# Forget terms in attention: a broadcast row added on the vector engine, or terms of the score product

## The chip, the cores and the metric

One core of one Trainium2 chip runs the whole program. Its engines work from queues of their own and meet through semaphores: TensorE (PE; its weight loads are listed apart as PEld), VectorE (DVE), ScalarE (ACT), GpSimd (POOL) and SyncE (SP), which here issues every DMA. The metric is device time in microseconds (us) for one execution, as the median of several executions. Lower is better.

## The reference

Attention with forget terms for 8 batches of 8 heads, 576 positions, 64 features per head, and behind it a channel mix over 512 features with 1024 hidden ones.

```
s_pos = np.maximum(s, 0.0)
cum = np.cumsum(s_pos, axis=-1)
bias = -(cum[:, :, :, None] - cum[:, :, None, :])
scores = np.where(causal, -1000000000.0, scores + np.minimum(bias, 0.0))
scores = scores - np.max(scores, axis=-1, keepdims=True)
attn = np.exp(scores)
attn = attn / (np.sum(attn, axis=-1, keepdims=True) + 1e-09)
...
xk = mu_k * x + (1.0 - mu_k) * x_prev
xr = mu_r * x + (1.0 - mu_r) * x_prev
k = np.maximum(xk @ w_k, 0.0)
v = k * k @ w_v
r = 1.0 / (1.0 + np.exp(-(xr @ w_r)))
return (r * v).astype(np.float32)
```

`scores` is q times k over the square root of 64. Of the bias a row of scores needs only the part of the key, `cum[key]`: the part of the query is the same along the row and falls out when the row's maximum is taken off. Below the diagonal `min(bias, 0)` is the bias itself. The weights w_k, w_v and w_r arrive as 64-bit floats.

## The kernel before

**The work.** A visit is a pair of heads of one batch. The 576 queries of a head are cut into five tiles: tile 0 has 64 queries, tiles 1 to 4 have 128 each, and tile t sees 64, 192, 320, 448 or 576 keys (QS, QN and KN in the code). Batch 0 goes in two rounds: the four pairs with tiles 0 to 2, which are the first 320 queries (visits of kind A), then the four pairs with tiles 3 and 4 (kind Z). Batches 1 to 7 take all five tiles at once; from batch 3 on two half tiles share a transpose (kind `Paired`, where `front` shifts the columns of tiles 2 and 4 by 64).

**A head.** `scores` makes the products of a tile into one of two PSUM banks `s`. In the first four visits this is a plain float32 product with one term (L719, two instructions each). Behind that the operands are split in two fp32r parts: G holds q's high part over its low part, KH is k's high part twice, KL its low part, and two products, KH by G and KL by G, add up (L730). Tile 4 is wider than a bank and goes in two halves of 288 keys. Then DVE adds the forget row, scales, and keeps the row's minimum of the negated scores (L757, each with a read of its accumulator). It does so in two kinds of pieces: keys left of the diagonal block take the row `cb`, which a DMA has spread from `cum_d` in DRAM over 128 partitions (L682, 288 KB a head), and keys of the diagonal block take `mask`, which POOL makes from `cb` with affine selects (L701). That is 5 pieces for an A head, 5 for a Z head and 10 for a head of all tiles. ACT takes the exponential and its sum (L775), POOL normalises (L791), PE transposes (L837), ACT and DVE split the transposed weights (L866, L870), PE multiplies with v (L986 in the plain visits, L1000 behind).

**The first rows.** `first_sums` spreads s of two heads over all partitions and runs two scans on DVE (L496); `prefix_sums` scans all 64 heads at once (L472) and writes `cum_d`; two DMAs of 480 KB spread the rows of six more heads.

**Loads.** SP loads q and k of each head twice, once for each half of the partitions (L630). ACT and POOL make the parts: KH (L645), KL (L649), G (L656, L660).

**The channel mix** runs over 18 chunks of 256 positions: mixing (L1104, L1111), splits xh and xl (L1133, L1137), hidden products (L1165), gates (L1207), outputs (L1232). Chunk 0 needs the A rounds of all four pairs. Its weights are turned from 64-bit to 32-bit floats and split on ACT, DVE and POOL, in 20 blocks of 512 KB (L548 to L579), spread over the first 110 us.

**The order.** All tasks are recorded with their reads and writes, priced, and put in an order by `Plan`: a list schedule over all engines by due times, twenty passes, the best one kept. So a changed task moves its neighbours too. While PE would idle before the first split score product, `Plan` fills it with small products of the identity (L398).

## Time and profile before

| What | Value |
|---|---|
| median of 3 runs | 860.07 us (859.77 to 861.87) |
| the profiled execution's own time | 860.73 us |
| its span, first to last instruction | 858.9 us |
| granted TensorE clock, mean | 0.998 |
| PE busy | 844.9 us, 98% of the span |
| DVE, ACT, POOL busy | 676.3, 679.2, 494.5 us |
| DMA | 109.04 MB, mean 127 GB/s |

Sums of the prediction are made against the profiled execution (860.73 us around a span of 858.9). A windows row gives a stretch, its length, then for PE, PEld, DVE, ACT and POOL the busy time and number of instructions, the granted clock, the share of time the 16 DMA engines moved data, and GB/s. A timeline row gives start, duration, engine, line, operation, output and inputs. The ends of matmuls are modelled, so a busy PE may still lose some time between them.

### The profile page before, as it was taken

What the parts mean: (1) busy time and instruction counts of PE and PEld (TensorE: products, weight loads), DVE (VectorE), ACT (ScalarE), POOL (GpSimd) and SP (SyncE); (2) the same over time, 40 slices, a digit from 0 to 9 for tenths busy, and PEclk for the clock granted to TensorE, in tenths of its full rate; (3) what the DMA queues carried; (4) which work ended last, traced back from release to release, by engine and by line L of the source; (5) the groups of instructions that cost most, each with busy time, mean ns of one, the idle gap of its engine ahead of it and who ended that gap; (6) DMA issues with size and microseconds to landing.
All of it is one profiled execution on the core that took longest, in us unless ns stands there. A gap on an engine that the chain in (4) does not pass through costs nothing.

```text
span 858.9 us, 18405 instructions
## 1 busy us (share of the span) xinstructions
PE 844.9 (98%) x5541; PEld 748.7 (87%) x5541; DVE 676.3 (79%) x2425; ACT 679.2 (79%) x1850; POOL 494.5 (58%) x854
## 2 busy tenths in 40 slices
PE   9979999999999999999999999999999999999998
PEld 8659789889898898989898989898989989988996
DVE  6988889989877998789878887888888789455431
ACT  3998999999988898789979797978897878445331
POOL 5897899997766757466665566456665652000000
PEclk9999999999999999999999999999999999999999
DMA  8879655564443545335343435252534220210100
GB/s 249 257 236 265 192 164 166 166 184 141 148 136 111 144 124 156 96 112 158 110 128 118 136 104 158 77 149 84 168 98 135 86 92 15 64 33 18 50 26 24
DMA packets 63108, 109.04 MB, mean 127 GB/s; under 512 B 10144, under 2 KB 24480, under 8 KB 63008
## 3 DMA queue, kind: packets, MB, share of 16 engines
q1 hardware_dynamic: 63008, 107.87, 42.7%
q8 instruction: 43, 0.70, 0.3%
q14 instruction: 57, 0.47, 0.2%
HBM read 88.80 MB, written 19.04 MB: 126 GB/s over the span
## 4 chain that ended last, share of the span: by engine, by line
PE 91%; ACT 3%; DMA 2%; DVE 1%; issue 1%; POOL 1%; SPq 0%; ACTq 0%; POOLq 0%; DVEq 0%
PE m L1232 21%; PE m L1165 19%; PE s L730 10%; PE m L1207 10%; PE po L1000 9%; PE t L837 9%; PE t L1232 2%; PE po L398 2%; PE po L986 2%; PE s L1165 2%; PE t L1165 2%; PE t L1000 1%; PE t L937 1%; PE s L719 1%; DMA w_v<-in_moe_w_v 1%
## 5 line engine op out<-in xcount | busy, mean ns | idle before, releaser
L1165 PE MATMUL m<-xh,w_k 128*128 128x256 f32 x976 | 200.3, 286 | 0.0
L775 ACT ACTIVATE W<-W,nm 128x448 f32<-128x448 f32 (+4 forms) x320 | 179.9, 563 | 25.2 <-DVE nm L757 22.4
L1232 PE MATMUL m<-w_v,kh 128*128 128x512 f32 x528 | 188.1, 406 | 0.0
L791 POOL TENSOR_SCALAR W<-W,rinv 64x64 f32<-64x64 f32 (+4 forms) x320 | 164.3, 532 | 12.6 <-DVE rinv L820 10.6
L1165 PEld LDWEIGHTS m<-xh,w_k 128*128 128x128 f32 x976 | 158.8, 189 | 1.4 <-DVE kl L1194 0.2
L837 PE MATMUL t<-ident,W 128*128 128x128 f32 (+1 forms) x736 | 134.7, 276 | 6.4 <-ACT ph L866 2.7
L1165 PE MATMUL m<-xl,w_k 128*128 128x256 f32 x488 | 139.7, 286 | 0.0
L649 POOL TENSOR_TENSOR KL<-raw,KH 128x576 fp32r<-128x576 f32 x64 | 91.6, 1432 | 80.1 <-ACT KH L645 75.4
L870 DVE TENSOR_TENSOR pl<-t,ph 128x512 fp32r<-128x512 f32 x224 | 107.1, 485 | 12.7 <-ACT ph L866 10.7
L837 PEld LDWEIGHTS t<-ident,W 128*128 128x128 f32 (+1 forms) x736 | 89.3, 137 | 27.0 <-ACT ph L903 5.2
L1232 PEld LDWEIGHTS m<-w_v,kh 128*128 128x128 f32 x528 | 98.1, 189 | 15.3
L730 PE MATMUL s<-KH,G 128*64 128x64 f32 (+2 forms) x360 | 110.7, 312 | 0.3 <-DVE nm L757 0.3
L757 DVE CUSTOM_DVE_ANT_0 W<-s,cb 128x64 f32<-128x64 f32 (+1 forms) x244 | 92.1, 381 | 17.9 <-PE s L730 15.4
L1232 PE MATMUL m<-w_v,kl 128*128 128x512 f32 x264 | 105.7, 400 | 0.0
L730 PE MATMUL s<-KL,G 128*64 128x64 f32 (+3 forms) x360 | 105.5, 297 | 0.0
L866 ACT CAST ph<-t 128x512 fp32r<-128x512 f32 x224 | 93.1, 424 | 12.5 <-PE t L837 10.5
L660 POOL TENSOR_TENSOR G<-raw,G 64x576 fp32r<-64x576 f32 (+1 forms) x64 | 85.8, 1341 | 27.6 <-issue 10.2
L1111 DVE SCALAR_TENSOR_TENSOR xp<-x,mu,xp 128x256 f32<-128x256 f32 (+3 forms) x184 | 76.3, 415 | 25.0 <-ACT xp L1104 22.5
L1104 ACT ACTIVATE xp<-x,mu 128x256 f32<-128x256 f32 (+3 forms) x184 | 77.6, 422 | 21.4 <-DMA x<-x_d 12.1
L1165 PEld LDWEIGHTS m<-xl,w_k 128*128 128x128 f32 x488 | 92.2, 189 | 0.8 <-DVE xl L1137 0.3
L1207 PE MATMUL m<-w_r,xh 128*128 128x512 f32 x264 | 92.6, 402 | 0.0
L757 DVE CUSTOM_DVE_ANT_0 W<-s,mask,nm 128x128 f32<-128x128 f32 x256 | 86.7, 344 | 3.1 <-POOL mask L701 0.5
(154 smaller groups left out, 1934.0 us busy)
## 6 DMA issues: line engine op xcount, KB each, us to landing
raw<-in_k SPq DMA_DIRECT2D x128, 144.0 KB, 3.2
cb<-cum_d SPq DMA_DIRECT2D x64, 288.0 KB, 3.6
raw<-in_q SPq DMA_DIRECT2D x112, 144.0 KB, 3.7
out<-g SPq DMA_DIRECT2D x36, 256.0 KB, 2.6
vn<-in_v SPq DMA_DIRECT2D x28, 320.0 KB, 3.3
x_d<-xT SPq DMA_DIRECT2D x28, 288.5 KB, 2.5
x<-x_d SPq DMA_DIRECT2D x11, 514.0 KB, 4.6
w_k<-in_moe_w_k SPq DMA_DIRECT2D x8, 512.0 KB, 5.5
```

The lines of the kernel that those rows point to most:

```text
L649: lambda k=k, kh=kh, kl=kl: nc.gpsimd.tensor_tensor(out=kl.get(), in0=k.get(), in1=f32(kh.get()), op=ALU.subtract),
L730: lambda x=x, K=K: nc.tensor.matmul(ps.get()[:m, :w], G.get()[:, q0 : q0 + m], K.get()[:, k0 : k0 + w], start=x == 0, stop=x == 1,),
L757: lambda a=a, e=e, row=row, i=i, to=to: nc.vector.tensor_tensor_reduce(out=to(), in0=ps.get()[:m, a - k0 : e - k0], in1=row()[:m, a:e], sc ...
L775: lambda: nc.scalar.activation(W.ap[:m, :n], W.ap[:m, :n], AF.Exp, bias=nm.get()[:m, 3 * t + mi : 3 * t + mi + 1], scale=-1.0, accum_out=s ...
L791: lambda: nc.gpsimd.tensor_scalar(out=to.ap[:m, c : c + n], in0=W.ap[:m, :n], scalar1=rinv.get()[:m, t : t + 1], scalar2=1.0, op0=ALU.mult ...
L837: lambda: nc.tensor.transpose(ps.get()[0:m, place : place + P], pt[t].ap[:, k0 + front(t, tiles) : k0 + front(t, tiles) + m], ident.ap,),
L866: act(lambda: nc.scalar.copy(strips(ph), src()), [ps], [(ph, k) for k in ks], n * m)
L870: lambda: nc.vector.tensor_tensor(out=strips(pl), in0=src(), in1=f32(strips(ph)), op=ALU.subtract),
L1000: lambda: nc.tensor.matmul(po.get()[: P if both else 64, at + q0 - base : at + q0 - base + m], V.get()[:, kb, 2 * j : 2 * j + (2 if both e ...
L1165: lambda u=u, f=f, c=c, n=n, w=w, x=x: nc.tensor.matmul(ps.get()[:, u * CT : (u + 1) * CT], weight["k", c, f // 4].get()[:, w, f % 4 * P : ...
L1207: lambda c=c, n=n, x=x, w=w: nc.tensor.matmul(ps.get(), x.get()[:, c, ts], weight["r", c, 0].get()[:, w], start=c == 0 and n == 0, stop=c ...
L1232: lambda f=f, n=n, x=x, w=w: nc.tensor.matmul(ps.get(), x.get()[:, f, ts], weight["v", f, 0].get()[:, w], start=f == 0 and n == 0, stop=f ...
```

## The change

The forget row is no longer added from SBUF by DVE. In the first four visits (the first 320 queries of batch 0) PE adds it to the score: products whose weights are one head's forget terms, one column of them repeated, and whose moving operand is `till`, a triangle of ones (L739 in the changed kernel). A tile of w keys takes two such products (the high and the low part) for each block of 128 keys: 2, 4 and 6 for tiles 0, 1 and 2, so 12 for an A head and 96 in all. For the rest the running sums of all heads are cut into three fp32r parts and kept in DRAM (`cum3_d`), and three rows of them are loaded under k's 64 rows, against three rows of ones under the low part of q. The two score products are now K by QQ (q's high part twice, k's high and low part) and KB by QL (64 rows of k, rounded, and the 3 rows), with 67 rows in the second (L761). So there are as many score products as before.

With the forget term in the sum, DVE adds only a fixed table, `lower` (zeros, and a triangle of large negative numbers), and takes a tile in one piece (L779): 3 pieces for an A head, 3 for a Z head, 6 for a head of all tiles and 8 for a Paired one. The selects on POOL, the rows `cb` and `mask`, and the spreading DMAs go. k is loaded once for both heads of a pair. A copy of 64 rows of k to KB (L703) comes to DVE, one for each of the 64 split heads (the Z and the full ones), and a DMA of 3 rows for each (L687). At the start come five memsets, two subtractions of 64x576 on DVE and two casts of 64x576 on ACT. The planner's constants are unchanged.

```diff
-    cum_d = fixed(dram.tile([B * H, S], F32, name="cum_d"))
+    cum3_d = fixed(dram.tile([B * H, 3, S], F32, name="cum3_d"))
+    lower = fixed(const.tile([P, S], F32, name="lower"))
...
+        parts = [sbuf([B * H, S], x, 1, F32R) for x in ("w_v_2_0", "w_v_3_0", "xh1")]
+        for i, x in enumerate(parts):
+            if i < 2:
+                act(lambda x=x: nc.scalar.copy(x.get(), cum.get()), [cum], [x], S, 90)
+                dve(
+                    lambda i=i, x=x: nc.vector.tensor_tensor(
+                        out=(parts[2] if i else cum).get(), in0=cum.get(), in1=f32(x.get()),
+                        op=ALU.subtract,
+                    ),
+                    [cum, x], [parts[2] if i else cum], S,
+                )
+            dma(
+                lambda i=i, x=x: nc.sync.dma_start(cum3_d.ap[:, 2 - i], f32(x.get())),
+                [x], [(cum3_d, i)], 410,
+            )
...
+    def early_sums():
...
+        till = sbuf([P, n], "xh0", 1, F32R)
+        one = sbuf([P, n], "xl1")
+        rows = sbuf([P, nb, H], "r")
+        parts = sbuf([P, 2, nb, H], "xl0", 1, F32R)
...
+        dve(lambda: nc.vector.memset(one.get(), 1.0), [], [one], n)
+        pool(
+            lambda: nc.gpsimd.affine_select(
+                out=one.get(), in_=one.get(), pattern=[[1, n]], base=0, channel_multiplier=-1,
+                compare_op=ALU.is_ge, fill=0.0,
+            ),
+            [], [one], n, 137,
+        )
...
+            own, other = slice(64 * j, 64 * j + 64), slice(64 - 64 * j, P - 64 * j)
+            QQ, K = (sbuf([P, n], x, 3, F32R) for n, x in ((nq, "G"), (nk, "KH")))
+            QL, KB = (sbuf([P, S], x, 3, F32R) for x in ("QL", "KL"))
+            if made[0] < 3:
+                made[0] += 1
+                ahead(lambda QL=QL: nc.vector.memset(f32(QL.get()[64:67]), 1.0), (QL, 1), S)
+            dma(
+                lambda j=j, KB=KB: nc.sync.dma_start(
+                    f32(KB.get()[64:67, 0:nk]), cum3_d.ap[b * H + 2 * hp + j, :, 0:nk]
+                ),
+                [(cum3_d, i) for i in range(3)], [(KB, 1)], 40,
+            )
...
+                lambda own=own, other=other, K=K: nc.gpsimd.tensor_tensor(
+                    out=K.get()[other], in0=k.get()[own], in1=f32(K.get()[own]), op=ALU.subtract
+                ),
+                [(k, j), (K, j)], [(K, 1 - j)], nk, 210, 2.21, (2 * j, 2 - 2 * j),
+            )
+            dve(
+                lambda own=own, KB=KB: nc.vector.tensor_copy(KB.get()[0:64, 0:nk], k.get()[own]),
+                [(k, j)], [(KB, 0)], nk, 1.92, 150, (2 * j, 0),
+            )
...
+                lambda x=x, QQ=QQ, QL=QL: nc.gpsimd.tensor_tensor(
+                    out=QL.get()[0:64, 0:nq], in0=x.get()[0:64], in1=f32(QQ.get()[0:64]),
+                    op=ALU.subtract,
+                ),
+                [(x, 0), (QQ, 0)], [(QL, 0)], nq, 210, 2.21,
+            )
+            found.append(((QQ, K, P), (QL, KB, 67)))
+        return found
...
-            CB, part = sbuf([P, NK], "cb", 2), 0
-            bias_row = CB.get
-            dma(
-                lambda: nc.sync.dma_start(
-                    CB.get(), cum_d.ap[b * H + h : b * H + h + 1, 0:NK].broadcast_to([P, NK])
-                ),
-                [cum_d], [CB], 819 * NK / S,
-            )
...
-            pool(
-                lambda: nc.gpsimd.affine_select(
-                    out=own(M.get),
-                    in_=own(bias_row),
-                    pattern=[[-1, m]] if n == 1 else [[0, n], [-1, m]],
-                    base=0,
-                    channel_multiplier=1,
-                    compare_op=ALU.is_ge,
-                    fill=MASK * ISCALE,
-                ),
-                [(CB, part)], [(M, k0 > 0)], n * m, 137,
-            )
...
+                parts, till = bias
+                for kb in range(-(-w // P)):
+                    for x in range(2):
+                        pe(
+                            lambda kb=kb, x=x: nc.tensor.matmul(
+                                ps.get()[:m, P * kb : w],
+                                parts.get()[:, x, kb, h : h + 1].broadcast_to([P, m]),
+                                till.get()[:, 0 : w - P * kb],
+                                start=kb == x == 0,
+                                stop=False,
+                            ),
+                            [(parts, x), till], [ps], w - P * kb, m,
+                        )
...
-            for x, K in enumerate((KH, KL) if KL is not None else ()):
+            for x, (G, K, n) in enumerate(() if plain else passes):
                 y = pe(
-                    lambda x=x, K=K: nc.tensor.matmul(
+                    lambda x=x, G=G, K=K, n=n: nc.tensor.matmul(
                         ps.get()[:m, :w],
-                        G.get()[:, q0 : q0 + m],
-                        K.get()[:, k0 : k0 + w],
+                        G.get()[:n, q0 : q0 + m],
+                        K.get()[:n, k0 : k0 + w],
                         start=x == 0,
                         stop=x == 1,
...
-            for a, e in ((k0, min(k0 + w, QS[t])), (max(k0, QS[t]), k0 + w)):
+            off = S - P - QS[t] if QS[t] < k0 + w else -k0
+            last = k0 + w - (f if QS[t] < k0 + w else 0)
+            for a, e, to in ((k0, last, k0 + f), (last, k0 + w, 0)):
                 if a >= e:
                     continue
-                own = a >= QS[t]
-
-                def to(a=a, e=e, own=own):
-                    x = W.ap[:m, a + f : e if own else e + f]
-                    if not (own and f):
-                        return x
-                    return bass.AP(
-                        tensor=x.tensor, offset=x.offset, ap=[x.ap[0], [-P * t, 2], [1, 64]]
-                    )
-
-                bias, row = (M, M.get) if own else (CB, bias_row)
                 dve(
-                    lambda a=a, e=e, row=row, i=i, to=to: nc.vector.tensor_tensor_reduce(
-                        out=to(),
+                    lambda a=a, e=e, to=to, i=i: nc.vector.tensor_tensor_reduce(
+                        out=W.ap[:m, to : to + e - a],
                         in0=ps.get()[:m, a - k0 : e - k0],
-                        in1=row()[:m, a:e],
+                        in1=lower.ap[:m, off + a : off + e],
...
-            loaded[n] = load_turned(q, b, hp, q0, q1), load_turned(k, b, hp, 0, q1)
+            loaded[n] = load_twice(b, hp, q0, q1), load_keys(b, hp, q1, "raw", 4)
...
+    ahead(lambda: nc.vector.memset(lower.ap, 0.0), lower, S)
+    pool(
+        lambda: nc.gpsimd.affine_select(
+            out=lower.ap[:, S - P : S], in_=lower.ap[:, S - P : S], pattern=[[-1, P]], base=0,
+            channel_multiplier=1, compare_op=ALU.is_ge, fill=MASK * ISCALE,
+        ),
+        [], [lower], P, 137,
+    )```

Three places where the order changes. The first is PE's queue in the A rounds; s is a PSUM bank of scores, t one of transposes, xh and xl hold the triangle and the forget terms, KH and kl or kh hold k and q, and ident is the identity. Before:

```order
L837 MATMUL t_418<-ident,W_72 64x128
L719 MATMUL s_218<-KH_125,kh_105 64x64
L837 MATMUL t_418<-ident,W_72 64x128
L986 MATMUL po_87<-ph_143,V_290 128x64
L837 MATMUL t_413<-ident,W_72 128x128
L719 MATMUL s_213<-KH_125,kh_105 128x192
```

And now:

```order
L739 MATMUL s_146<-xh_112,xl_138 128x320
L739 MATMUL s_146<-xh_112,xl_138 128x192 x2
L739 MATMUL s_146<-xh_112,xl_138 128x64 x2
L750 MATMUL s_146<-KH_179,kl_123 128x320
L856 MATMUL t_316<-ident,W_72 128x128 x2
```

Each score product has the running sums ahead of it in its bank, and the first ones of a bank can stand well ahead of the product.

The second is DVE's queue in the first Z heads; cb and mask are the forget rows, W the scores, m and xp banks in which weights are turned, and KL what the changed kernel calls KB. Before:

```order
L757 ISA W_0_71,nm0_241<-s1_213,cb0_162 128x288
L757 ISA nm0_241 128x1
L571 SCALAR_TENSOR_TENSOR xh10_256<-w_r_0_00_610,xp0_325 128x512
L820 RECIPROCAL rinv1_423<-rinv1_423 128x3
L757 ISA W_0_71,nm0_241<-s0_218,cb0_162,nm0_241 128x160
L757 ISA nm0_241 128x1
L757 ISA W_0_71,nm0_241<-s0_218,mask0_184,nm0_241 128x128
L757 ISA nm0_241 128x1
```

And now:

```order
L839 RECIPROCAL rinv1_313<-rinv1_313 128x3
L703 CAST KL0_569<-raw3_433 64x576
L582 TENSOR_SCALAR xp0_307<-xp0_307 128x512
L779 ISA W_1_72,nm1_254<-s1_146,lower_77 64x64
L779 ISA nm1_254 64x1
L589 TENSOR_SCALAR xp0_307<-xp0_307 128x512
L779 ISA W_1_72,nm1_254<-s0_143,lower_77 128x192
L779 ISA nm1_254 128x1
```

A piece of 160 and one of 128 keys are gone as separate instructions, and the copy L703 stands between pieces of the A heads, in front of steps that turn weights (L582, L589).

The third is PE's queue where chunk 0 begins. Before, 18 split score products stand ahead of chunk 0's first hidden product, and the first half of chunk 0's inputs (w_k of rows 0 and 1) follows in one piece:

```order
L730 MATMUL s0_218<-KH0_762,G2_792 128x288
L730 MATMUL s0_218<-KL2_833,G2_792 128x288
L1165 MATMUL m0_197<-xh00_845,w_k_0_00_268 128x256
L1165 MATMUL m0_197<-xl00_851,w_k_0_00_268 128x256
L1165 MATMUL m0_197<-xh00_845,w_k_0_00_268 128x256
L1165 MATMUL m0_197<-xh00_845,w_k_1_00_351 128x256
```

Now 14 stand ahead of it:

```order
L761 MATMUL s1_146<-KH0_683,G2_690 128x288
L856 MATMUL t1_310<-ident_66,W_0_71 128x128
L1184 MATMUL m0_197<-xh00_112,w_k_0_00_344 128x256
L856 MATMUL t0_316<-ident_66,W_0_71 128x128 x3
L1184 MATMUL m0_197<-xl00_138,w_k_0_00_344 128x256
L1184 MATMUL m0_197<-xh00_112,w_k_0_00_344 128x256
```

Chunk 0's first products moved ahead of transposes and score products of the Z heads.

More of the change, by code (lines that the diff above doesn't have):

```diff
@@ new lines, in early_sums @@
+    def early_sums():
+        n = KN[A[-1]]
+        nb = -(-n // P)
+        till = sbuf([P, n], "xh0", 1, F32R)
+        one = sbuf([P, n], "xl1")
+        rows = sbuf([P, nb, H], "r")
+        parts = sbuf([P, 2, nb, H], "xl0", 1, F32R)
+        dma(
+            lambda: nc.sync.dma_start(
+                rows.get(), s_t[0, 0 : nb * P].rearrange("(k p) h -> p k h", p=P)
+            ),
+            [], [rows], 100,
+        )
+        dve(lambda: nc.vector.memset(one.get(), 1.0), [], [one], n)
[6 more added lines that the diff above has]
+        )
+        act(lambda: nc.scalar.copy(till.get(), one.get()), [one], [till], n, 90)
+        act(
+            lambda: nc.scalar.activation(rows.get(), rows.get(), AF.Relu, scale=ISCALE),
+            [], [rows], nb * H, 94,
+        )
+        act(lambda: nc.scalar.copy(parts.get()[:, 0], rows.get()), [rows], [(parts, 0)], nb * H, 90)
+        dve(
+            lambda: nc.vector.tensor_tensor(
+                out=parts.get()[:, 1], in0=rows.get(), in1=f32(parts.get()[:, 0]), op=ALU.subtract
+            ),
+            [rows, (parts, 0)], [(parts, 1)], nb * H,
+        )
+        return parts, till
@@ L635, in load_turned, with ahead @@
         return xs
-    def split_qk(qs, ks):
-        nq, nk = qs[0].n, ks[0].n
-        G = [sbuf([P, nq], "G", 3, F32R) for _ in range(2)]
-        KH, KL = ([sbuf([P, nk], x, 3, F32R) for _ in range(2)] for x in ("KH", "KL"))
-        for j in range(2):
-            k, kh, kl = ks[j], KH[j], KL[j]
-            act(
-                lambda k=k, kh=kh: nc.scalar.copy(kh.get(), k.get()),
-                [(k, 0), (k, 1)], [(kh, 0), (kh, 1)], nk, 90,
+    made = [0]
+    def ahead(emit, what, n):
+        due, plan.due = plan.due, -2.0e5
+        dve(emit, [], [what], n)
+        plan.due = due
@@ new lines, in split_qk @@
+    def split_qk(b, hp, qs, k):
+        nq, nk = qs[0].n, k.n
+        found = []
+        for j in range(2):
+            own, other = slice(64 * j, 64 * j + 64), slice(64 - 64 * j, P - 64 * j)
[10 more added lines that the diff above has]
+            )
+            act(
+                lambda own=own, K=K: nc.scalar.copy(K.get()[own], k.get()[own]),
+                [(k, j)], [(K, j)], nk, 90,
@@ L722, in products @@
                         KH.get()[:, k0 : k0 + w],
-                        start=True,
+                        start=False,
                         stop=True,
@@ L766, in products @@
                     ),
-                    [ps, (bias, t > 0 if own else part)] + ([(nm, (t, i - 1))] if i else []),
+                    [ps, lower] + ([(nm, (t, i - 1))] if i else []),
                     [(W, i), (nm, (t, i))], e - a, extra=143 if i else 78,
@@ L803, in rs @@
             return x.get()[:, tiles[0] : tiles[-1] + 1]
-        if 0 in tiles:
-            mask(64, 0, 1)
-        mask(P, QS[max(1, tiles[0])], len([t for t in tiles if t]))
         for t in tiles:
@@ L1313, in forgetting_attention_then_channel_mix @@
     plan.due = -2.0e5
[L1314 removed]
+    bias = early_sums()
     prefix_sums()
[L1316 to L1326 removed]
     QKs, Vs, early_x = {}, {}, []
@@ L1433 @@
     for name in _INS:
-        a = inputs[name]
+        a = inputs[name.removesuffix("_t")]
+        if name == "s_t":
+            a = a.transpose(0, 2, 1)
         if name in ("q", "k"):
```

86 lines of the change are left out of this document (19 added, 67 removed).

## The prediction

> **What bounds the kernel now.** I read the head of the page first, then the windows by stage, then the chain of waits for prices.
>
> ```profile
> span 858.9 us, 18405 instructions
> PE 844.9 (98%) x5541; PEld 748.7 (87%) x5541; DVE 676.3 (79%) x2425; ACT 679.2 (79%) x1850; POOL 494.5 (58%) x854
> ...
> 0.00:20.00 20.00, 18.18 (x175) 16.64 (x176) 12.56 (x37) 7.72 (x18) 9.90 (x37) 1.00 0.83 239
> 20.00:61.00 41.00, 33.85 (x192) 24.28 (x189) 37.68 (x139) 38.78 (x125) 36.55 (x72) 0.96 0.81 250
> 61.00:90.00 29.00, 28.92 (x195) 25.79 (x195) 24.36 (x68) 26.16 (x64) 23.45 (x29) 1.00 0.97 263
> 90.00:112.00 22.00, 21.52 (x119) 16.68 (x117) 18.90 (x74) 21.30 (x59) 19.91 (x31) 1.00 0.60 171
> 112.00:230.00 118.00, 117.97 (x814) 105.48 (x813) 107.93 (x448) 114.46 (x326) 103.63 (x179) 1.00 0.56 164
> 230.00:700.00 470.00, 469.33 (x3107) 422.12 (x3105) 392.55 (x1474) 398.71 (x1103) 291.78 (x491) 1.00 0.42 122
> 700.00:845.00 145.00, 145.00 (x909) 129.81 (x908) 80.99 (x191) 72.02 (x162) 9.26 (x21) 1.00 0.12 38
> ```
>
> From 112 to 845 us PE stands still for 0.7 of 733 us, at full clock. There the time is the number of columns that PE streams, and a lighter DVE, POOL or DMA buys nothing. The head is another stage: from 20 to 61 us PE is busy for 33.85 of 41, while ACT has 38.78 and DVE 37.68. And part of PE's work in the head is filler; these are the windows of the filler's line alone:
>
> ```profile
> 0.00:20.00 20.00, 15.67 (x159) 14.61 (x160) 1.00 0.83 239
> 20.00:61.00 41.00, 3.98 (x32) 2.63 (x30) 0.96 0.81 250
> ```
>
> So to 61 us, where chunk 0 begins, PE does 18.18 + 33.85 - 15.67 - 3.98 = 32.4 us of real work and has 28.6 us free. Turning the weights and the A rounds on ACT and DVE set the pace. The change has to be priced twice: as PE work wherever PE is full, and as ACT, DVE, POOL and DMA work in the head.
>
> **PE: score products behind the A rounds.** Their number and columns stay, 720 as before; the contraction is 67 rows in every second one. What a column costs is read from long runs of equal products on the chain (start, time, what):
>
> ```profile
> 114.47 0.87 PE t L837 x8
> ...
> 829.87 5.68 PE s L1165 x48
> 843.98 11.18 PE t L1232 x48
> ```
>
> 256 columns take 118 ns and 512 take 233, both with 128 rows, so 0.45 ns a column and some 3 ns an instruction. No row shows a product with 67 rows. The nearest, the two groups of the present score products,
>
> ```profile
> L730 PE MATMUL s<-KH,G 128*64 128x64 f32 (+2 forms) x360 | 110.7, 312 | 0.3 <-DVE nm L757 0.3
> L730 PE MATMUL s<-KL,G 128*64 128x64 f32 (+3 forms) x360 | 105.5, 297 | 0.0
> ```
>
> differ by 15 ns a product, in favour of the second, for equal columns. I take 0 and bound it by 360 x 15 ns = 5.4 us either way, which I think far too wide. Each product has its own weight load before and now, so the second operand adds no loads.
>
> **PE: 96 products of running sums.** An A head has 2 of 64, 2 x (192 + 64) and 2 x (320 + 192 + 64) columns, 1792 in 12 products; eight heads 14336 in 96. That is 14336 x 0.45 + 96 x 3 ns = 6.7 us. Where the small ones are held up by their weight loads, the row of eight transposes above bounds them: each has a load of its own and takes 109 ns, so 96 x 109 ns = 10.5 us at most. I take 6.7, since most columns lie in long products. It lies at about 7 to 50 us, in the 28.6 us that PE has free; the cover is ACT and DVE. If PE were full there it would cost 6.7. On the path: 0, bounds 0 and +6.7. What is queued behind a product that waits for its bank is the transposes and v products of the heads before, as the first piece of order shows.
>
> **DVE.** A piece costs its start-to-start distance:
>
> ```profile
> 5.86 0.50 DVE L465 TENSOR_SCALAR mask<-mask 64x576 f32<-64x576 f32 x1 [5.86 <-DMA mask<-in_s]
> 6.29 0.80 DVE L496 TENSOR_TENSOR_SCAN cb<-raw,raw 128x320 f32<-128x320 f32 x1
> ...
> 18.47 0.35 DVE L757 CUSTOM_DVE_ANT_0 W<-s,cb 128x192 f32<-128x192 f32 x1
> ...
> 18.74 0.34 DVE L757 CUSTOM_DVE_ANT_0 W<-s,mask,nm 128x128 f32<-128x128 f32 x1
> ...
> 19.02 0.35 DVE L757 CUSTOM_DVE_ANT_0 W<-s,mask,nm 128x128 f32<-128x128 f32 x1
> ...
> 41.96 0.47 DVE L757 CUSTOM_DVE_ANT_0 W<-s,cb 128x320 f32<-128x320 f32 x1
> 42.37 0.07 DVE L757 DVE_READ_ACCUMULATOR2_ANT nm<- 128x1 f32 x1
> ```
>
> 192 and 128 keys take 0.27 + 0.28 us, one piece of 320 takes 0.41: a merge saves 0.14. In the head there are 2 merges in each of 16 A and Z heads and 4 in about two full heads: 40 x 0.14 = 5.6 us. Against it stand the copies L703, twelve by the time the last weights are turned (counted in the order). Of one element for one, 64x576, the row above takes 0.43 us start to start. The weight steps of 128x512 take 0.68 us, which is the upper bound. So 12 x 0.43 = 5.2, up to 8.2. Net -0.4, bounds -0.4 and +2.6. Two scans of 0.80 go and five memsets and two subtractions come, about as much as that and 2 us more by the same rows; they stand before 20 us, where DVE has 7.4 us free. Behind 112 us DVE loses or gains a fraction of a us per head under a full PE: nothing.
>
> **ACT, POOL, DMA.**
>
> ```profile
> L649 POOL TENSOR_TENSOR KL<-raw,KH 128x576 fp32r<-128x576 f32 x64 | 91.6, 1432 | 80.1 <-ACT KH L645 75.4
> L701 POOL TENSOR_SCALAR_AFFINE_SELECT mask<-cb 64x64 f32<-64x64 f32 (+1 forms) x124 | 50.9, 427 | 16.0 <-DMA cb<-cum_d 10.1 <-DVE cb L496 3.7 <-DVE nm L757 0.3
> L645 ACT CAST KH<-raw 128x576 fp32r<-128x576 f32 x64 | 43.0, 672 | 1.4 <-DMA raw<-in_k 0.9 <-PE s L730 0.6
> ...
> PEld t L837 <- POOL W L791: 1.6, 3, 0.8
> PE t L837 <- POOL W L791: 0.9, 2, 0.6
> ...
> DMA packets 11577, 22.68 MB, mean 252 GB/s; under 512 B 1820, under 2 KB 5959, under 8 KB 11566
> raw<-in_k SPq DMA_DIRECT2D x20, 144.0 KB, 4.8
> cb<-cum_d SPq DMA_DIRECT2D x8, 288.0 KB, 5.6
> w_v<-cum_d SPq DMA_DIRECT2D x2, 480.0 KB, 7.2
> ```
>
> ACT gets two casts of 64x576 (0.67 each, bound by the row above) and three small ones, before 20 us, where it has 12 us free: 0. Its casts of k have half the partitions and as many columns: 0. POOL's two subtractions keep their columns (L649, L660); the selects go, in the head 16 A and Z heads with some 24 selects of 0.43 us or less, about 8 us of its 70 from 20 to 112. PE's direct waits for POOL from 20 to 61 us are the row of 0.9, and I give the change these 0.9 us. Of the 22.68 MB that move up to 90 us, 8 x 288 + 2 x 480 KB of rows and half of 20 x 144 KB of k go, 4.7 MB. SP has fewer issues to make and is past nothing that it was not past before. The transfers are hidden where engines set the pace: 0, bounds 0 and -5 (below).
>
> **The order.** Chunk 0's first product stands behind 14 split score products rather than 18, among transposes of the Z heads. PE then has something to do while ACT and DVE finish the rest of chunk 0's inputs. But the Z work comes later and has to be done under a full PE. I count this as nothing.
>
> **The sum.** 860.7 + 0 (running sums, hidden) + 0 (score products) - 0.4 (DVE) - 0.9 (POOL) = **859.4 us**. The profiled execution is 0.7 above the median of the runs; I leave it, since the bounds are wider.
>
> **Rivals.**
>
> The head gets shorter. For it: DMA is at a share of 0.81 to 0.97 up to 90 us, and the chain runs through transfers from 66.65 to 79.72 us:
>
> ```profile
> 66.65 6.69 DMA w_v<-in_moe_w_v
> 73.35 6.37 DMA raw<-in_k
> ```
>
> 4.7 MB at 252 GB/s are 19 us of transfers. Against it: ACT is idle for only 2.2 us from 20 to 61 and 0.7 from 90 to 112, DVE for 3.3 and 3.1. Half the idle time of both (9.3) is 4.7, so **856**.
>
> The running sums are not hidden. Place: A rounds, about 10 to 50 us, two `s` banks. A bank is now held through up to 7 products ahead of DVE's piece; DVE and ACT, full at 92 and 95%, wait, and chunk 0 starts later. For it: the chain in the A rounds alternates between all engines, PE among them. Against it: the order puts sums well ahead of their product. It decides once a wait on a bank falls on DVE; with all of 6.7 us exposed it gives 867, with most of it **865**.
>
> The copy on DVE and POOL's work shut each other out. POOL is busy 36.55 of 41 us, in pieces of 1.43 us and less, so a copy that could not run beside POOL would meet a piece nine times in ten and wait some 0.5 us for its rest: 12 x 0.5 = 6 us more on DVE in the head. It has 3.3 + 4.6 + 3.1 us free there, so about half would come through: **862 to 864**. In this trace DVE has hardly an operation of this kind (L465, once), so nothing shows it. The Trainium skill speaks against the change here: its page "SBUF — State Buffer", section "Who interferes with whom", says that a copy or cast of VectorE in a two-port mode and a GpSimd instruction lock each other out for a whole instruction; by that rule this case would be the one that comes.
>
> The change doesn't do what it says: half of PE's score operands change place, and a score product with 67 rows may be slower; 360 x 15 ns would give 866. Little speaks for it.
>
> **Numbers.** Forecast, hidden and nearly neutral, 857 to 862: 0.47. Shorter head, 856: 0.28. Sums exposed: 0.13. Lock: 0.10. Slower product: 0.02. About 0.3%, that is 2.6 us, can be told from no change here. The forecast gives 0.05 of its chance to faster and 0.02 to slower; so faster 0.33, within 0.40, slower 0.27. The range leaves out the far ends of the first and second rival: 854 to 865.5.
>
> **What would show it.** Hidden: the filler shrinks by about as much as L739 takes (from 19.7 us), and chunk 0's first product stays near 61 us or earlier. A full PE from about 112 us with windows as above confirms the rest; the score line L761 should keep its mean times. The exposed case shows as DVE waiting for PE at L779 before 50 us. The lock shows as L703 well over 0.5 us, or as POOL's subtractions longer than 1.43. The shorter head shows as chunk 0 at 57 us or less. I am wrong in kind if the stretch behind 112 us changes its length by more than 2 us.

## The result, and the profile after

The changed kernel takes 872.06 us (median; 871.47 to 872.61) against 860.97 for the kernel before on the same chip: a ratio of 1.0126, interval 1.0102 to 1.015. It is slower by about 11 us. Its profiled execution has a span of 869.7 us, 10.8 more than before.

The head of its page, and the chain of waits by engine and by line, with the chain by engine of the kernel before behind them:

```profile
span 869.7 us, 17512 instructions
PE 851.7 (98%) x5519; PEld 751.0 (86%) x5519; DVE 698.5 (80%) x2143; ACT 688.4 (79%) x1854; POOL 449.5 (52%) x719
...
PE 76%; DVE 12%; ACT 8%; issue 3%; DMA 1%; SPq 0%; POOL 0%; ACTq 0%; DVEq 0%
PE m L1251 16%; PE m L1184 16%; PE m L1226 9%; PE s L761 8%; PE po L1019 7%; PE t L856 7%; DVE W L779 3%; ACT W L797 3%; DVE KL L703 2%; DVE pl L889 2%; PE t L1251 2%; PE po L1005 2%; PE s L1184 2%; PE t L1184 2%; PE s L750 1%
```

```profile
PE 91%; ACT 3%; DMA 2%; DVE 1%; issue 1%; POOL 1%; SPq 0%; ACTq 0%; POOLq 0%; DVEq 0%
```

DVE now stands in the chain with 12%, for 1% before, and the copies L703 with 2% by themselves. DVE has fewer instructions than before (2143 for 2425) and is busy 22 us longer. The stages (the columns are those of the windows shown before), and the filler's line alone:

```profile
0.00:20.00 20.00, 17.98 (x140) 16.17 (x141) 16.80 (x48) 12.74 (x40) 10.42 (x41) 1.00 0.88 246
20.00:61.00 41.00, 37.77 (x247) 31.30 (x246) 39.91 (x105) 39.92 (x120) 35.32 (x53) 1.00 0.77 243
61.00:90.00 29.00, 29.00 (x187) 25.55 (x186) 27.51 (x64) 27.88 (x65) 22.77 (x30) 1.00 0.53 163
90.00:112.00 22.00, 20.93 (x117) 16.22 (x114) 16.20 (x46) 19.88 (x54) 18.87 (x27) 1.00 0.33 99
112.00:230.00 118.00, 115.32 (x794) 102.28 (x793) 109.05 (x354) 112.44 (x318) 88.93 (x142) 1.00 0.34 104
230.00:700.00 470.00, 464.71 (x3040) 412.95 (x3038) 399.22 (x1318) 396.43 (x1079) 260.29 (x403) 1.00 0.28 85
700.00:845.00 145.00, 145.00 (x900) 129.16 (x901) 85.01 (x205) 75.04 (x177) 12.91 (x27) 1.00 0.12 40
```

```profile
0.00:20.00 20.00, 6.81 (x56) 5.73 (x56) 1.00 0.88 246
20.00:61.00 41.00, 1.90 (x15) 1.26 (x15) 1.00 0.77 243
```

To 61 us PE does 17.98 + 37.77 - 6.81 - 1.90 = 47.0 us of work that is not filler; before it was 32.4. Of the 14.6 us about 7 are the running sums, which are new work (7.3 us less idle time with them than without them, in the windows further below); the rest is a head start. From 112 to 700 us PE stands still for 2.68 + 5.29 = 8.0 us; before it was 0.7. So the head got ahead, and the full stage lost it and more. Standing still is only part of that loss: from 112 to 700 us PE starts about 3830 products in place of 3920. At 588 us for 3920 the missing ones are some 13 us (an estimate, since the products differ in size and the two kernels do not do the same work there), so some of the loss seems to lie within time that the profile counts as busy. The source views of the chunks' hidden products, of before and of after, say the same with their first and last start:

```profile
L1165 PE MATMUL m<-xh,w_k x976: 274/281/467, 61.5 to 774.9; 128*128 128x256 f32 x196
```

```profile
L1184 PE MATMUL m<-xh,w_k x976: 274/281/471, 50.4 to 785.5; 128*128 128x256 f32 x196
```

The first begins 11 us earlier, the last 11 us later. What stands behind PE's gaps from 112 to 700 us is in the waits of PE (us in total, times, longest), in the source view of the copies (nanoseconds: shortest, median, longest) and in the groups of the score products and the copies:

```profile
PE po L1019 <- DVE pl L889: 3.2, 7, 0.8
PE t L856 <- DVE xT L1057: 1.8, 4, 0.5
PE t L856 <- DVE pl L943: 1.4, 3, 0.5
PE t L1019 <- DVE pl L889: 0.8, 2, 0.4
PE m L1226 <- DVE kl L1213: 0.5, 1, 0.5
```

```profile
L703 DVE CAST KL<-raw x64: 417/518/2062, 33.5 to 698.3; 64x576 fp32r<-64x576 f32 x64
```

```profile
L761 PE MATMUL s<-KH,G 128*64 128x64 f32 (+1 forms) x360 | 108.7, 309 | 0.5 <-DVE nm L779 0.5
L761 PE MATMUL s<-KL,QL 67*64 67x64 f32 (+1 forms) x360 | 106.1, 299 | 0.0
L703 DVE CAST KL<-raw 64x576 fp32r<-64x576 f32 x64 | 50.1, 784 | 1.0
```

PE waits for DVE in every row. The same 64x576 copy takes 0.42 us or 2.06, 0.78 on average. The score products have their old mean times. Their ends are modelled, but their starts agree: from the start of one with 67 rows and 288 columns to the next start on PE it is 135 ns in the median, and 133 ns with 128 rows before. So the one with 67 rows is not slower. One long copy in the timelines of DVE, POOL and PE (start, time, what; in brackets the idle time before it):

```profile
244.10 2.06 DVE L703 CAST KL<-raw 64x576 fp32r<-64x576 f32 x1
246.09 0.86 DVE L889 TENSOR_TENSOR pl<-t,ph 128x384 fp32r<-128x384 f32 x2
...
244.02 1.42 POOL L712 TENSOR_TENSOR QL<-raw,G 64x576 fp32r<-64x576 f32 x1 [0.64 <-ACT G L708]
245.41 1.77 POOL L813 TENSOR_SCALAR W<-W,rinv 128x192 f32<-128x192 f32 x3
...
246.67 0.42 PE L1019 MATMUL po<-pl,V 128*64 128x448 f32 x1 [0.81 <-DVE pl L889]
```

The copy stands while POOL's subtraction L712 runs and the first of the three L813 behind it, which ends at 245.85 us in the trace; the copy ends 0.31 us later. Behind it on DVE wait the pieces L889 of the transposed weights, and PE's product L1019 waits for them, 0.81 us. This is the rule and not one case: all 28 copies of over 0.6 us in this trace end 0.31 or 0.32 us behind the end of a POOL instruction, and the 12 that met no POOL instruction took 0.44 to 0.46 us. At 0.45 us the 64 copies would take 28.8 us. They take 50.1: 21.3 us on DVE are waiting. POOL is held up too: its subtraction L697 took up to 1.71 us here, and at most 1.44 in the run further below that has the copies on POOL.

### The profile page after: what moved, and what is told of

Its sections match the earlier page's. It is cut to its first block, busy times and chain, and to the rows that moved or that the text cites. A ratio compares the mean times of both kernels' runs of the same rounds, so it can differ in the third digit from the quotient of the medians.

```text
span 869.7 us, 17512 instructions
## 1 busy us (share of the span) xinstructions
PE 851.7 (98%) x5519; PEld 751.0 (86%) x5519; DVE 698.5 (80%) x2143; ACT 688.4 (79%) x1854; POOL 449.5 (52%) x719
## 4 chain that ended last, share of the span: by engine, by line
PE 76%; DVE 12%; ACT 8%; issue 3%; DMA 1%; SPq 0%; POOL 0%; ACTq 0%; DVEq 0%
PE m L1251 16%; PE m L1184 16%; PE m L1226 9%; PE s L761 8%; PE po L1019 7%; PE t L856 7%; DVE W L779 3%; ACT W L797 3%; DVE KL L703 2%; DVE pl L889 2%; PE t L1251 2%; PE po L1005 2%; PE s L1184 2%; PE t L1184 2%; PE s L750 1%
## 5 line engine op out<-in xcount | busy, mean ns | idle before, releaser
L1184 PE MATMUL m<-xh,w_k 128*128 128x256 f32 x976 | 205.5, 288 | 0.5 <-ACT xh L1152 0.3
L797 ACT ACTIVATE W<-W,nm 64x64 f32<-64x64 f32 (+4 forms) x320 | 179.6, 562 | 26.3 <-DVE nm L779 22.0
L1251 PE MATMUL m<-w_v,kh 128*128 128x512 f32 x528 | 187.6, 406 | 0.0
L813 POOL TENSOR_SCALAR W<-W,rinv 128x192 f32<-128x192 f32 (+4 forms) x320 | 166.7, 540 | 25.4 <-DVE rinv L839 23.8
L1184 PEld LDWEIGHTS m<-xh,w_k 128*128 128x128 f32 x976 | 160.2, 189 | 3.0 <-ACT xh L1152 0.7
L779 DVE CUSTOM_DVE_ANT_0 W<-s,lower 128x448 f32<-128x448 f32 (+5 forms) x320 | 130.1, 414 | 26.2 <-PE s L761 21.0
L1184 PE MATMUL m<-xl,w_k 128*128 128x256 f32 x488 | 138.9, 285 | 0.0
L856 PE MATMUL t<-ident,W 128*128 128x128 f32 (+1 forms) x736 | 134.0, 275 | 4.5 <-DVE xT L1057 1.8
L697 POOL TENSOR_TENSOR KH<-raw,KH 64x576 fp32r<-64x576 f32 x64 | 92.9, 1451 | 83.9 <-ACT KH L693 45.5
L889 DVE TENSOR_TENSOR pl<-t,ph 128x512 fp32r<-128x512 f32 x224 | 106.4, 484 | 11.9 <-ACT ph L885 9.9
L856 PEld LDWEIGHTS t<-ident,W 128*128 128x128 f32 (+1 forms) x736 | 89.5, 137 | 25.7 <-DVE xT L1057 2.8
L1251 PEld LDWEIGHTS m<-w_v,kh 128*128 128x128 f32 x528 | 97.9, 189 | 14.3 <-ACT g L1238 0.3
L761 PE MATMUL s<-KH,G 128*64 128x64 f32 (+1 forms) x360 | 108.7, 309 | 0.5 <-DVE nm L779 0.5
L761 PE MATMUL s<-KL,QL 67*64 67x64 f32 (+1 forms) x360 | 106.1, 299 | 0.0
L1251 PE MATMUL m<-w_v,kl 128*128 128x512 f32 x264 | 106.0, 402 | 0.0
L1226 PE MATMUL m<-w_r,xh 128*128 128x512 f32 x264 | 95.1, 406 | 0.5 <-DVE kl L1213 0.5
L712 POOL TENSOR_TENSOR QL<-raw,G 64x576 fp32r<-64x576 f32 (+1 forms) x64 | 86.6, 1353 | 13.3 <-ACT G L708 11.2
L1184 PEld LDWEIGHTS m<-xl,w_k 128*128 128x128 f32 x488 | 92.4, 189 | 0.9
L632 POOL TENSOR_TENSOR V<-vn,V 128x320 fp32r<-128x320 f32 x56 | 48.4, 882 | 70.9 <-ACT V L628 64.5
```

Of the source, the lines that this page charges most:

```text
L697: lambda own=own, other=other, K=K: nc.gpsimd.tensor_tensor(out=K.get()[other], in0=k.get()[own], in1=f32(K.get()[own]), op=ALU.subtract),
L712: lambda x=x, QQ=QQ, QL=QL: nc.gpsimd.tensor_tensor(out=QL.get()[0:64, 0:nq], in0=x.get()[0:64], in1=f32(QQ.get()[0:64]), op=ALU.subtract,),
L761: lambda x=x, G=G, K=K, n=n: nc.tensor.matmul(ps.get()[:m, :w], G.get()[:n, q0 : q0 + m], K.get()[:n, k0 : k0 + w], start=x == 0, stop=x == 1,
L779: lambda a=a, e=e, to=to, i=i: nc.vector.tensor_tensor_reduce(out=W.ap[:m, to : to + e - a], in0=ps.get()[:m, a - k0 : e - k0], in1=lower. ...
L797: lambda: nc.scalar.activation(W.ap[:m, :n], W.ap[:m, :n], AF.Exp, bias=nm.get()[:m, 3 * t + mi : 3 * t + mi + 1], scale=-1.0, accum_out=s ...
L813: lambda: nc.gpsimd.tensor_scalar(out=to.ap[:m, c : c + n], in0=W.ap[:m, :n], scalar1=rinv.get()[:m, t : t + 1], scalar2=1.0, op0=ALU.mult ...
```

## Experiments

Two theories stood against each other after that. **The copies:** DVE's copies and POOL's instructions shut each other out, and the late DVE pieces open gaps under a full PE. **Something else:** the order, the running sums, or the bytes.

**The copy elsewhere.** The copies go to POOL, to ACT, or to a transfer out of the rounded keys; the planner is told each time.

```diff
-            dve(lambda ...: nc.vector.tensor_copy(KB[0:64, 0:nk], k[own]), ...)
+            pool(lambda ...: nc.gpsimd.tensor_copy(KB[0:64, 0:nk], k[own]), ...)   # or
+            act(lambda ...: nc.scalar.copy(KB[0:64, 0:nk], k[own]), ...)           # or
+            dma(lambda ...: nc.sync.dma_start(KB[0:64, 0:nk], K[own]), ...)
```

> The copies L703 run on POOL instead of DVE; everything else as in the changed kernel. Theory (the copies on DVE and POOL's instructions hold each other up, and the late DVE pieces open gaps on PE): the copies on POOL take a steady time, the many PE gaps between 112 and 700 us go, and the 16 us that are lost there come back: 872 - 16 = 856, within 853 to 860. Rival (the loss has another cause: the running sums, the order, the 67-row products): no DVE piece of importance is lighter by more than 0.4 us a head, so 870 to 873.

> The copies run on ACT instead of DVE. Theory of the lock: the copies take a steady time of about 0.5 to 0.7 us, which ACT has to spare behind 230 us but not in the head; the gaps behind 112 us go, and the time is 856 to 864. Rival (another cause): 870 to 874.

> The copy is made by a transfer from the first 64-row half of the rounded keys, so no engine does it. PE's own work is 801.7 us, and what is lost beside it was 64.1 us in the kernel before, 68.0 in the changed one, 64.6 with the copy on POOL. Theory A (the copy, wherever an engine makes it, is what costs between 100 and 700 us): the loss there falls from 28 to the 20 us of the kernel before, the shorter head stays, and the time is 853 to 860. Theory B (what the head gains is given back behind it whatever makes the copy, and the 6.9 us of running sums come on top): the loss stays at 63 to 66 us and the time is 865 to 868.

Measured: 867.37 us on POOL (1.0073, interval 1.005 to 1.0095), 870.18 on ACT (1.0098, 1.0083 to 1.0113), 866.56 by transfer (1.0056, 1.0038 to 1.0075). All are slower than before. On POOL and by transfer they are faster than the changed kernel's 1.0126 (1.0102 to 1.015); on ACT the intervals overlap. The first lies between what theory and rival expected, the second at its rival's, the third at theory B's. ("PE's own work" in the last expectation is an estimate: every product but the filler, priced by its columns at about the rates that the prediction reads from the chain; what is lost is the span less that. The 16 us of the first expectation are an estimate too, more than the 8.0 that PE stands still.) Each of these kernels has another order as well, since the planner makes it anew. That had to be separated.

**The planner told the truth, and the copy in the kernel before.**

```diff
 changed kernel:  [(k, j)], [(KB, 0)], nk, 1.92, 150 -> 484
 kernel before:   + dve(lambda k=k: nc.vector.tensor_copy(k[0:64], k[0:64]), [], [(k, 0)], nk, 1.92, 150)
```

> The copies stay on DVE, but the planner is told 784 ns for one, their mean in the profile of the changed kernel, instead of 450. If the loss comes from the order, in which pieces stand too close behind a copy that is planned too short, most of the 16 us come back: 857 to 864. If the DVE time and the unforeseeable length of a single copy (417 to 2062 ns) are what costs, little comes back: 868 to 873.

> The kernel before, with one DVE copy of 64x576 added for each head whose keys are split (64 in all, the raw keys copied onto themselves, nothing else changed). Theory of the lock: the copies take 0.4 to 2 us beside POOL's work, the stretch from 112 to 700 us gets PE gaps, and the time rises by 8 to 20 us, to 869 to 880. Rival (the copies are harmless, the loss of the changed kernel lies elsewhere): copies of about 0.43 us and 860 to 862.

Measured: 868.25 us (1.0073, 1.0056 to 1.009) with the dearer copy, 0.5% less than the changed kernel and at the lower end of the second range, with copies that take as long as ever (809 ns on average); and 884.07 (1.0259, 1.0242 to 1.0276), above the whole range, for the kernel before with 64 copies, of 802 ns. So copies cost time in either kernel, but these runs change the order too.

**Other orders of the same work.** One constant of the planner, the pause it assumes when an engine's next instruction lies in other partitions, is changed; no instruction is added or taken.

```diff
-    SWITCH = 20.0
+    SWITCH = 25.0      # e7, e8, e12; 15.0 in e16
```

> The kernel before with one constant of the planner changed (the pause it assumes when an engine changes its place in memory, 20 ns, now 25), so the same instructions in another order. If orders of equal merit on paper differ little on the chip: 860 to 863. If the order before was a lucky one, as large as what is sought: 864 to 870.

> The kernel before with 15 in place of 20 ns for the planner's pause, a third order of the same work. If the order before is a lucky one among its like: 864 to 869, as the second (865.7). If the second was an unlucky one: 860 to 863.

> The copy by transfer with the same change of the planner's constant. If orders differ little: within 2 us of the copy by transfer. If the order is a matter of luck: 3 us or more away, either way.

> The changed kernel, copies on DVE, in the order that comes of 25 ns in place of 20 for the planner's pause. If the changed kernel met an unlucky order: 866 to 869. If its copies cost what is lost: 870 to 876.

Measured: the kernel before 865.72 us (1.0053, 1.0038 to 1.0068) and 867.51 (1.0066, 1.0051 to 1.0081); the copy by transfer 867.87 (1.0076, 1.0059 to 1.0093); the changed kernel 877.73 (1.0185, 1.017 to 1.02). So the order of the kernel before is better than both of its neighbours, by 4.6 and 5.7 us, and the changed kernel's is no unlucky one beside its one neighbour tried, which is slower still and above both ranges. The copy by transfer moves by only 1.3 us, too little to be told from none. In the windows of 112 to 700 us, first before, then its second order:

```profile
112.00:700.00 588.00, 587.30 (x3920) 527.60 (x3918) 500.48 (x1919) 513.17 (x1428) 395.41 (x669) 1.00 0.44 130
```

```profile
112.00:700.00 588.00, 583.96 (x3888) 522.97 (x3887) 496.46 (x1903) 511.13 (x1415) 394.30 (x668) 1.00 0.44 130
```

PE stands still for 0.7 us in the one and 4.0 in the other. A change that makes the planner start anew gives up that order.

**The order held.** Here the planner's input is untouched, and only what is issued differs: the copy goes to POOL in the place where it was planned on DVE. Three pairs: the changed kernel's order, the order of the dearer copy, and the order of the 25 ns pause.

```diff
-            dve(lambda ...: nc.vector.tensor_copy(KB[0:64, 0:nk], k[own]), ...)
+            dve(lambda ...: nc.gpsimd.tensor_copy(KB[0:64, 0:nk], k[own]), ...)
```

> The changed kernel with its order untouched (the planner still believes that DVE makes the copy), but the copy is issued to POOL, where it takes 0.66 us every time. If the uneven copies on DVE are what the changed kernel loses between 112 and 700 us: 862 to 867, as with a planned copy on POOL (867) or better. If the order alone costs it: 871 to 874.

> The order that the planner makes when it is told 784 ns for the copy, with the copy then issued to POOL. A second pair for the price of the copies on DVE at an unchanged order (with DVE: 868.3). If DVE's copies are what costs there too: 860 to 864. If their price depends on the order and is small in this one: 867 to 869.

> The order of the changed kernel with 25 ns for the planner's pause (877.7 with the copies on DVE), the copy issued to POOL and nothing else moved. A third pair for the price of the copies. If the price depends on what the planner was told (450 ns, as in the first pair, 7.8 us; the pair with 784 ns gave 1.4): 867 to 871. If it varies with the order at random: anywhere from 866 to 877.

Measured, as ratios to the kernel before:

| order of | copy on DVE | copy on POOL | apart |
|---|---|---|---|
| the changed kernel (copy told as 450 ns) | 1.0126 (1.0102 to 1.015) | 1.0032 (1.0021 to 1.0044), 864.27 us | 0.94%, 8.1 us |
| 25 ns pause (450 ns) | 1.0185 (1.017 to 1.02) | 1.0049 (1.0034 to 1.0064), 865.88 us | 1.36%, 11.7 us |
| dearer copy (784 ns) | 1.0073 (1.0056 to 1.009) | 1.0054 (1.0038 to 1.0071), 866.84 us | 0.19%, not told from none |

The copies on POOL in the changed kernel's order, and PE's stage with them:

```profile
L703 POOL CAST KL<-raw x64: 655/662/677, 34.9 to 692.4; 64x576 fp32r<-64x576 f32 x64
```

```profile
112.00:700.00 588.00, 584.67 (x3873) 521.93 (x3872) 480.25 (x1639) 512.68 (x1412) 383.13 (x610) 1.00 0.30 90
```

Each takes 0.66 us, longer than a free copy on DVE, but evenly; PE stands still for 3.3 us in place of 8.0. In the chain of this kernel DVE is back at 2%. The first two pairs show what the copies on DVE cost where they are planned too short: their plain time and their waiting together. In the pair of the dearer copy they take as much of DVE, 51.8 us, and the price is not seen: PE stands still for 4.4 us from 112 to 700 us with the copies on DVE and for 5.6 with them on POOL. In that order, then, the load on DVE alone is not what costs. It is one pair, and that the planner then keeps urgent pieces from standing behind a copy is only argued. The second pair, at 865.88 us, came out just below what was expected.

**What shuts what out.** In the kernel before, with the order kept on every engine, one DVE instruction is issued with each cast of keys, unknown to the planner: a copy of 64x576, or an addition of 64x288 with both inputs in SBUF, which takes as long (0.41 us at the least, both).

```diff
+   nc.vector.tensor_copy(kl[0:64], k[0:64])                                        # e10
+   nc.vector.tensor_tensor(out=kl[0:64, 0:288], in0=k[0:64, 0:288], in1=k[0:64, 288:576], op=add)   # e11
```

> The kernel before with its order untouched on PE, ACT, POOL and SP; behind each of the 64 casts of keys one DVE copy of 64x576 is issued that the planner knows nothing of (raw keys to the place that POOL's subtraction fills next). If copies on DVE cost time through what they hold up: copies of 0.4 to 2 us, mean about 0.8, and 868 to 878. If the 22 us of the planned copies came from the new order: 861 to 865.

> The same with a DVE addition of two halves of the keys (64x288, some 0.45 us by the rows of such pieces) in place of the copy: as much DVE work, another kind of instruction. If only the copy's kind is held up by POOL: pieces of a steady 0.45 us and 861 to 865. If any extra DVE piece at this place costs as much: the same time as with the copy.

Measured: 895.18 us (1.0383, 1.0359 to 1.0406) and 895.88 (1.04, 1.0384 to 1.0415), both far above the 868 to 878 that were expected. The source views of the copy and of the addition, and then a subtraction of the kernel before, L1137, whose one input lies in a PSUM bank:

```profile
L645 DVE CAST KL<-raw x64: 413/452/3916, 31.2 to 720.6; 64x576 fp32r<-64x576 f32 x64
```

```profile
L645 DVE TENSOR_TENSOR KL<-raw x64: 409/450/3924, 31.4 to 720.7; 64x288 fp32r<-64x288 f32 x64
```

```profile
L1137 DVE TENSOR_TENSOR xl<-xp,xh x72: 641/686/694, 54.3 to 822.1; 128x512 fp32r<-128x512 f32 x72
```

My expectation that only a copy is held up fell: the addition is held up as long, while L1137 with one input in SBUF never is (694 ns at most, though 51 of the 72 ran beside POOL's work). The Trainium skill has this: its page "SBUF — State Buffer", section "Who interferes with whom", says that a VectorE instruction with two SBUF inputs contends with a GpSimd instruction that reads SBUF, and one with at most one such input outside the two-port modes does not. The addition and L1137 agree; the copy, with one input in SBUF, is the case that the prediction cites from the same section.

The 34 us are more than the 8 to 12 of a planned copy. PE's waits from 112 to 700 us in the run with the copy, and what POOL's next subtraction waits for:

```profile
PE s L730 <- DVE nm L757: 4.6, 5, 1.6
PE t L837 <- DVE pl L870: 4.4, 4, 3.4
PE po L1000 <- DVE pl L870: 4.2, 3, 3.4
PE t L1000 <- DVE pl L870: 2.4, 1, 2.4
PE t L837 <- DVE xT L1038: 1.4, 1, 1.4
```

```profile
its engine sat idle before it (us, times) until:
  ACT KH L645: 53.0, 16
...
  DVE KL L645: 4.7, 3
```

PE stands still for 19.2 us there, 17.0 of them for late DVE pieces: the order was planned without the 55.7 us that the copies take on DVE. POOL's subtraction waits only 4.7 us for the copies; its 53.0 us for ACT's cast of keys are less than in the kernel before (75.4). The mean granted clock is also lower, 0.989 for 0.998; how much of the 34 us that makes was not separated.

**The running sums.** Without the 96 products, once in a new order (with the copy by transfer) and once in the changed kernel's (with the copy on POOL). Both leave out the forget term of the first 320 queries of batch 0.

```diff
-   pe(lambda ...: nc.tensor.matmul(ps[:m, P * kb : w], parts[...], till[...], start=kb == x == 0, ...), ...)
+   pe(lambda: None, ...)      # e13; in e6 the call is gone; the score product starts the bank
```

> As the copy by transfer, and without the 96 products of the running sums: it leaves out the forget term of the first 320 queries of batch 0. If the sums are hidden in the head: the same time as with them, within 1 us. If PE's work counts one for one, wherever it lies: 6 to 8 us less.

> The changed kernel's order, the copy on POOL as in the run with the order untouched, and the 96 products of running sums not issued (it leaves out the forget term of the first 320 queries of batch 0); all else in the same place. If the sums are hidden in the head: 863 to 865, as with them (864.3). If they are on the path in full: 864.3 - 6.9 = 857.4; in part, between.

Measured: 867.69 us (with them 866.56) and 864.53 (with them 864.27; 1.0034, 1.0022 to 1.0046). The sums cost nothing that can be told here (about 1 us). The windows with them and without them, in the changed kernel's order with the copy on POOL:

```profile
0.00:20.00 20.00, 18.11 (x135) 16.33 (x135) 16.01 (x44) 12.13 (x37) 10.38 (x40) 1.00 0.80 228
20.00:61.00 41.00, 37.47 (x243) 30.54 (x241) 36.84 (x102) 39.51 (x120) 36.58 (x56) 1.00 0.77 238
...
230.00:700.00 470.00, 468.82 (x3076) 418.99 (x3075) 380.00 (x1299) 399.34 (x1091) 286.27 (x450) 1.00 0.29 86
```

```profile
0.00:20.00 20.00, 15.06 (x98) 11.11 (x98) 16.57 (x48) 12.71 (x40) 10.54 (x41) 1.00 0.85 240
20.00:61.00 41.00, 33.25 (x192) 24.37 (x191) 35.94 (x99) 39.58 (x120) 37.46 (x57) 1.00 0.78 241
```

To 61 us PE is idle for 5.4 us with the sums and for 12.7 without. So their time, 7.3 us, comes out of idle time.

**The bytes.** The changed kernel's order with the copy on POOL, and transfers to a spare place in DRAM behind those of keys and rows, of the size of what fell away; in the first run with three more at the start for the first rows.

```diff
+   nc.sync.dma_start(junk[...][:, 0:nk], cum3_d[...].broadcast_to([P, nk]))   # a head: 288 KB
+   nc.sync.dma_start(junk[...][:, 0:e], k[b, 2 * hp : 2 * hp + 2, ...])        # a pair
```

> The changed kernel's order with the copy on POOL, and as many bytes moved as in the kernel before: behind each transfer of rows or keys, one into a spare place in memory of the size of the one that fell away. If the head is shorter because it moves 4.7 MB less: the head loses most of the 11 us that PE gained to 100 us, and the time is 870 to 876. If the shorter head comes from the order and the fewer pieces on the engines: 864 to 867.

> As the run with the bytes put back, but without the three spare transfers of 1.3 MB ahead of the first inputs, which held up the start: some 3.4 MB up to 112 us and as much per head behind it as in the kernel before. If bytes set the pace of the head: PE loses 4 to 8 us more to 100 us than with the order untouched (28.0) and the time is 868 to 874. If only the late start cost those 21 us: 864 to 866.

Measured: 885.43 us (1.0275, 1.0253 to 1.0297) and 874.83 (1.0145, 1.0126 to 1.0164). The first lies above what was expected and is late from the start: DVE has 8.4 us of work in the first 20 and not 16. The second is the cleaner one; its windows:

```profile
0.00:20.00 20.00, 18.11 (x133) 16.30 (x133) 15.95 (x44) 11.87 (x36) 10.32 (x40) 1.00 0.83 231
20.00:61.00 41.00, 37.47 (x242) 30.60 (x242) 37.11 (x102) 39.52 (x119) 36.23 (x56) 1.00 0.90 292
...
230.00:700.00 470.00, 462.85 (x3038) 412.94 (x3036) 372.88 (x1273) 393.56 (x1074) 281.11 (x447) 1.00 0.41 122
```

PE's 18.11 and 37.47 us are the same to the last digit as without the added bytes, at 292 GB/s for 238. That is 16.6 MB to 61 us, more than the 15.0 of the kernel before, and chunk 0 begins at 52.1 us for 51.8 without the added bytes. So fewer bytes are not what makes the head shorter to 61 us. From 61 to 112 us PE does 1.2 us less than without them. The rest of some 10 us comes mostly from 230 to 700 us, where PE does 6.0 us less (468.82 without them), at a DMA share of 0.41, close to the 0.42 of the kernel before. There three transfers that nothing planned stand among the others on SP's queue for each pair of heads; whether it is their bytes or their place in the queue was not tried.

## Why the prediction was wrong, point by point

The time, 872.06, lies above the range. Two steps failed: the term for DVE behind 112 us, and the term for the order.

**"Behind 112 us DVE loses or gains a fraction of a us per head under a full PE: nothing."** This is the step that cost most. The load did grow by only a fraction of a us a head: DVE is busy for 508.3 us from 112 to 700 us, 7.8 more than before. But "nothing" does not follow. That PE stands still for 0.7 of 733 us was read as room on the other engines, and the order feeds PE just in time: in the timeline above one late DVE piece is a gap of 0.81 us. From 112 to 230 us DVE and ACT were nearly full, with 107.93 and 114.46 of 118 us; but 5.3 of the 8.0 us are lost from 230 to 700 us, where DVE had been busy for 392.55 of 470. What costs there, by PE's waits above, is a piece that comes late, however much DVE is idle elsewhere. Of the 11 us, 8.1 are the copies on DVE, by the pair with the order held.

**The lock, rival three,** was the right mechanism at 0.10, with the wrong place and so the wrong size. It was counted for the twelve copies in the head, half of them hidden. By the same working for all 64 copies it is far more: POOL is busy for 58% of the span, and half of one of its instructions of 1.4 us is 0.7, which gives an estimate of 64 x 0.58 x 0.7 = 26 us on DVE. Measured were 21.3. The prediction noted that DVE "has hardly an operation of this kind"; the row L1137 shows what that hid, a kernel in which the pieces that split and turn read one side from PSUM. The rule of the Trainium skill that was weighed there ("SBUF — State Buffer", "Who interferes with whom") agrees with the trace: copies of 0.42 to 2.06 us.

**The order: "I count this as nothing."** Wrong as a term: 0.32% (3 us) remain with the copies on POOL in the same order, and two neighbouring orders of the kernel before, with no other change, lie 0.53 and 0.66% above it. So the remainder is no more than what an order alone does here; that it is just this was not shown.

**The copies' time:** 0.43 us each nearly holds for one that meets nothing (0.44 to 0.46). With the waiting, the twelve to 112 us took 9.2 us for the 5.2 of the sum, above its bound of 8.2. The merges came out about as forecast: the score pieces take 26.3 us to 112 us in place of 32.6, 6.3 less for the 5.6 forecast. So the net was about +3 us on DVE in the head and not -0.4.

**Running sums, hidden:** right, 0 within what can be told (864.53 and 864.27). The filler shrank from 19.7 to 8.7 us, more than the 6.7 of the sums, as the head holds other work too.

**Score products:** right. 309 and 299 ns against 312 and 297, and equal distances of their starts; the rival of slower products with 67 rows is out.

**The head gets shorter (856):** half right. Chunk 0 begins at 50.4 us, earlier than the 57 named as its mark. But the gain does not reach the end; what the prediction said of the Z work, that it "has to be done under a full PE", fits this, though no run isolates it. The reason given for it, 4.7 MB less, does not hold to 61 us; what made the head shorter stays open.

**POOL -0.9 and ACT 0** are too small to be told from these runs. POOL's "70 from 20 to 112" are 79.9 by the windows shown, which changes no term. **What would show it** named the right marks: L703 "well over 0.5 us", POOL's subtractions "longer than 1.43", and a stretch behind 112 us that changes by more than 2 us.

No version beats the kernel before; the nearest is the changed kernel's order with the copy on POOL, 1.0032 of it.

## What to carry to other kernels

Before an operation is put on VectorE beside a busy GpSimd, look where its inputs lie: a copy, or an addition of two SBUF operands, of 0.45 us took 0.8 on average here and up to 3.9, while pieces with one input in PSUM kept their times. A full TensorE does not make the engines that feed it free, and even an engine with a sixth of its time idle delayed it here when single pieces came late: cost every piece added there by the time that it takes beside the other engines, and not by its time alone. In a kernel whose order a planner makes, hold the order and change only what is issued before a difference is put down to an operation; here the order alone was worth 4.6 to 5.7 us in the kernel before and in the changed one, and 1 to 2 us, too little to be told from none, in two variants of the changed one.

## What was not expected of the hardware

A held-up copy did not wait for one POOL instruction but for as many as POOL had standing one behind the other: for two in the timeline shown, and for five in the longest of the runs with the order of the kernel before, 3.9 us, more than twice the longest POOL instruction (1.7). Of the memsets of 128x1 on POOL, three of the six that fell beside the added copies took 0.36 to 0.41 us, while all six beside the added additions took 0.09 to 0.10 us, as they do alone. Casts on POOL of the same 64x576 took 0.66 us each time, within 22 ns.
